# Two decode layers of attention and mixer: a planned list of loads in place of a ring

## The chip, the cores and the metric

The kernel runs on one core of one Trainium2 chip. The time is device microseconds of one launch; that of the kernel before is 2558.41 us, the median of 3 runs (2557.43 to 2562.42).

A few words that are used below. A core has a matmul engine (TensorE, PE in the profile, with PEld for its weight loads), a vector engine (DVE), a scalar engine (ACT), GpSimd (POOL) and SyncE (SP), which here does little but issue DMAs. Sixteen DMA engines move the data between HBM and the on-chip memory, whose 128 partitions are the rows of every tile. Each engine works through its own list of instructions in order, and waits where an instruction needs something that another engine or a DMA has not delivered.

## What is computed

Two rows of 512 numbers (B = 2, one token each) pass through attention, a token mixer, attention and the mixer again, each with a layer normalisation before it and a residual sum behind it. Both attention layers read the same caches of keys and values.

```python
B, Sq, D = 2, 1, 512
Hq, Hkv, Sk, Dh = 32, 8, 32768, 128
...
def _A_ref(x, k_cache, v_cache, wq, wo):
    q = (x @ wq).reshape(B, Sq, Hq, Dh).transpose(0, 2, 1, 3)
    k = jnp.repeat(k_cache, rep, axis=1)
    v = jnp.repeat(v_cache, rep, axis=1)
    scores = jnp.einsum("bhqd,bhkd->bhqk", q, k) * (Dh ** -0.5)
    p = _softmax(scores, axis=-1)
    o = jnp.einsum("bhqk,bhkd->bhqd", p, v)
    return o.transpose(0, 2, 1, 3).reshape(B, Sq, Hq * Dh) @ wo

def _B_ref(x, w1, b1, w2, b2):
    h = _layernorm(x, axis=-1)
    u = _gelu(jnp.einsum("bsd,sf->bdf", h, w1) + b1)      # F = 1792
    return (jnp.einsum("bdf,fs->bds", u, w2) + b2).transpose(0, 2, 1)

x = A_x
x = x + _A_ref(_layernorm(x, axis=-1), A_k_cache, A_v_cache, A_wq, A_wo)
x = x + _B_ref(_layernorm(x, axis=-1), B_w1, B_b1, B_w2, B_b2)
x = x + _A_ref(_layernorm(x, axis=-1), A_k_cache, A_v_cache, A_wq, A_wo)
x = x + _B_ref(_layernorm(x, axis=-1), B_w1, B_b1, B_w2, B_b2)
```

All numbers are float32. K and V are 268 MB each, so a layer reads 537 MB.

## The kernel before

The work is cut into 32 **units**, one for each layer, batch and pair of K/V head (four query heads share one). A unit is named by layer, batch and head: (0, 1, 5). Its K and its V are 16.8 MB each. It is convenient to count in **cells** of 512 columns on 128 partitions (262,144 bytes): 64 cells of K and 64 of V for each unit. A cell is what one matmul reads as its moving side.

A unit goes through these steps. `make_q` projects the normalised row with the head's part of `wq` (8 cells hold one head's `wq` and `wo`) and turns the result into columns. `k_chunk` multiplies K's cells with them into the scores (two PSUM banks, one for each half of K). `max_1` and `max_2` find the maximum over all scores of each query head; `turn_scores` transposes one half (DVE), `exponentials` takes its four heads through ACT. `v_chunk` sums V's cells with these weights into `acc`. `denominators`, `out_1` and `out_2` divide and project with `wo` into the batch's `rows`. After the last unit of a layer and batch the mixer follows: `mix_1`, `take_rows`, `mix_2` (the sum and its normalisation), 14 times `hidden_tile` (a GELU of ACT and a projection of TensorE), `take_rows`, `mix_4`, and, after layer 0, `to_columns`, which leaves the row from which the next layer's queries are made.

Time is counted in chunks of 8 cells. In slot s of the last loop `load_k(s)` issues K's chunk s and TensorE works on it, and `load_v(s)` issues V's chunk of the unit before, ten slots behind (NCH + LAG). Most loads go through SP's queue, in the order of the code; the other steps are hung on the slots in `pre` and `post`.

`PAIRED` sets where two chunks come as one load of 4 MB (slots 0 to 47 and from 212 on), elsewhere a load is one chunk of 2 MB. All of it lies in one tile `mem`. Its first part is a ring of three places (RING); where loads are paired, the ring also takes room that holds weights later, or kept V earlier. The weights of all eight heads are loaded once and stay. `KEPT` leaves 18 cells of V of head 7 in memory from layer 0 to layer 1, for each batch in turn. In HBM a partition's row of K and of V is 32 KB long, of which a 2 MB load takes half.

Layer 1 of a batch can start only after the mixer of layer 0. The units are therefore ordered so that three units of the other batch lie between (BRIDGE), first of batch 1 in layer 0 and later of batch 0 in layer 1.

After the last V's pieces (8, 4, 2, 1 and 1 cells; the last two cells through narrow matmuls), `last_mixer` does the whole output and mixer of batch 1.

Of the kernel before, what the change touches and what calls it, by code (L numbers as in the profile page):

```python
# [8 lines left out]
F32 = mybir.dt.float32  # L9
# [17 lines left out]
QT = 4  # L27
DIRECT = 3
TAIL_GROUPS = (3, 3, 3, 2)
EPS = 1e-5  # L30


@with_exitstack
def gqa_mixer_kernel(ctx: ExitStack, tc: tile.TileContext, x, kt, v, wqo, cols, out):
# [4 lines left out]

    nc = tc.nc
    B, D = out.shape
    U, NCP, DH, _ = kt.shape  # L50
    NCH = 2 * NCP
    HKV = U // B
    R = wqo.shape[2] // (2 * D)
    DT = D // P
    FT = (cols.shape[1] - 1) // 3
    LAYERS = 2
    NU = LAYERS * U
    NT = NCH * JT
    HALVES = NCH // PACK
    SCALE = DH ** -0.5  # L60
    assert DH == P and R * PACK * SUB == 32 and PACK * SUB == 2 * QT and DT == NG and R == NG and D == 512
# [3 lines left out]
    hidden = ctx.enter_context(tc.tile_pool(name="hidden", bufs=1))  # L65
# [4 lines left out]


    xcols = const.tile([P, B, D // P], F32, name="xcols")
    nc.scalar.dma_start(xcols, x)


    W = wqo.shape[2] // 2
    RING0 = 0
    KEPT0 = RING0 + RING * CK
    kept_columns = sum(KEPT.values()) * QT * DH
    order = [HKV - 1] + list(range(HKV - 1))  # L80
    home = {h: KEPT0 + kept_columns + k * 2 * W for k, h in enumerate(order)}
    mem = const.tile([P, KEPT0 + kept_columns + HKV * 2 * W], F32, name="mem")
    kept = mem[:, KEPT0 : KEPT0 + kept_columns]
    wq_sb = [mem[:, home[h] : home[h] + W].rearrange("p (t c) -> p t c", t=DT) for h in range(HKV)]
    wo_sb = [mem[:, home[h] + W : home[h] + 2 * W].rearrange("p (t c) -> p t c", t=R) for h in range(HKV)]

    def load_weights(h):
        nc.sync.dma_start(mem[:, home[h] : home[h] + 2 * W], wqo[h])


    def places(base, k, size):
        return [base + (j % RING) * size for j in range(k, k + RING)]

    PLACES = (
        (PAIRED[0][0], [], places(RING0, 0, 2 * CK)),
        (PAIRED[0][1], [RING0 + j * CK for j in (2, 3, 4)], places(RING0, 0, CK)),
        (PAIRED[1][0], [], places(RING0, 2, 2 * CK)),
    )
    turn = {}

    def buffer(s, size):
        k = max(j for j in range(len(PLACES)) if PLACES[j][0] <= s)
        _, ahead, loop = PLACES[k]
        i = turn.get(k, 0)
        turn[k] = i + 1
        f = ahead[i] if i < len(ahead) else loop[(i - len(ahead)) % len(loop)]
        return mem[:, f : f + size]

    def paired(s):
        return any(a <= s < b for a, b in PAIRED)  # L110

    load_weights(0)
    cols_sb = const.tile([P, 3 * FT + 1], F32, name="cols_sb")
    nc.scalar.dma_start(cols_sb, cols)
# [3 lines left out]

    ident = const.tile([P, P], F32, name="ident")
    make_identity(nc, ident)  # L120
    one = const.tile([P, 1], F32, name="one")
    nc.gpsimd.memset(one, 1.0)
    ones = one.to_broadcast([P, P])
    half_neg = const.tile([P, 1], F32, name="half_neg")
    nc.gpsimd.memset(half_neg, -0.5)


    selg = const.tile([P, R * QT], F32, name="selg")
    nc.vector.tensor_reduce(
        selg, ident.rearrange("p (g r) -> p r g", g=NG)[:, : R * QT, :], axis=AX.X, op=ALU.add  # L130
    )

    sel1 = selg[:, 0:1].to_broadcast([P, P])
    qpad = [const.tile([P, 64], F32, name=f"qpad{k}") for k in range(2)]
    for t in qpad:
        nc.gpsimd.memset(t, 0.0)
# [3 lines left out]
    for t in rows:  # L140
        nc.vector.memset(t, 0.0)
# [59 lines left out]
    def unit_of(n):  # L201

        return units[n]
# [508 lines left out]
```

## Time and profile before

| what | value |
|---|---|
| time, median of 3 runs | 2558.41 us |
| profiled execution: its time, which is its span | 2557.4 us |
| mean granted TensorE clock | 0.806 |
| read from HBM, and its rate over the span | 1081.11 MB, 423 GB/s |
| TensorE busy | 1634.8 us |
| mean rate in the first and last of forty slices | 417 and 264 GB/s |

The page of the profile begins with the span and the busy time of each engine. A second part cuts the span into 40 slices and gives the engines' and the DMA's busy share of each in tenths. A third lists the DMA queues with packets, megabytes and the share of sixteen engines' time. A fourth follows back what ended last. A row of a group reads: line, engine, operation, tile written and read, shape, number of instructions, then busy time in us and mean duration of one in ns, then the time that the engine sat idle just before them and what ended it. A window's row gives, for a stretch of the span, the busy time of PE, PEld, DVE, ACT and POOL with their instruction counts, the clock, the DMA's share and the rate. A float32 matmul is recorded as two instructions.

### The profile page before, as it was taken

Reading aid. Unit: us, or ns where it says so; the run is one execution under the profiler, and the core shown is the slowest. Engines: PE = TensorE matmul, PEld = TensorE weight load, DVE = VectorE, ACT = ScalarE, POOL = GpSimd, SP = SyncE. Lnnn points to the kernel's source line nnn. Section 1 sums busy time; section 2 is a strip of 40 time slices with the busy share of each in tenths; the row PEclk is TensorE's granted clock in tenths of the full one; section 3 lists DMA queues with packets and bytes.
Section 4 is the critical chain, followed back from the end, with each engine's and each line's share of the span. In section 5 each row is a group of like instructions: output and inputs, shape, how many; then the busy total and the mean of one; then the engine's idle time right before and its main releaser. Section 6 shows DMA issues by size and latency. Waiting matters only on the chain.

```text
span 2557.4 us, 21623 instructions
## 1 busy us (share of the span) xinstructions
PE 1634.8 (64%) x9708; PEld 411.4 (16%) x9708; DVE 190.9 (7%) x487; ACT 201.8 (8%) x584; POOL 4.9 (0%) x17
## 2 busy tenths in 40 slices
PE   4556566666667666666666666666756766666656
PEld 1111111111111111111111111111111111111112
DVE  1000000000011000000000000001100100000001
ACT  0000000000012000000000000001200200000002
POOL 0000000000000000000000000000000000000000
PEclk8777877787898778878887778878888887677877
DMA  9999999999999999999999999999999999999996
GB/s 417 428 432 432 429 432 431 426 427 421 426 429 427 422 428 422 428 427 428 427 429 426 422 428 427 428 423 427 428 427 424 420 433 430 431 432 432 429 433 264
DMA packets 63174, 1082.52 MB, mean 423 GB/s; under 512 B 7269, under 2 KB 7273, under 8 KB 8170
## 3 DMA queue, kind: packets, MB, share of 16 engines
q1 hardware_dynamic: 62788, 1081.11, 99.3%
q8 instruction: 76, 1.25, 0.2%
q14 instruction: 16, 0.13, 0.0%
q10 hardware_dynamic: 294, 0.03, 0.0%
HBM read 1081.11 MB, written 0.00 MB: 423 GB/s over the span
## 4 chain that ended last, share of the span: by engine, by line
DMA 77%; PE 21%; issue 0%; DVE 0%; ACT 0%; SPq 0%; POOLq 0%; DVEq 0%; ACTq 0%
DMA mem<-in_v_dram 40%; DMA mem<-in_kt_dram 38%; PE acc L352 10%; PE scores L262 10%; PE misc L216 1%; PE misc L397 0%; PE acc L516 0%; PE misc L229 0%; ACT S L299 0%; PE rows L410 0%; PE misc L379 0%; DVE row L225 0%; PE bcast L492 0%; ACT mem L526 0%; PE rows L557 0%
## 5 line engine op out<-in xcount | busy, mean ns | idle before, releaser
L352 PE MATMUL acc<-mem,S 128*16 128x512 f32 x4092 | 683.6, 801 | 416.5 <-DMA mem<-in_v_dram 416.3
L262 PE MATMUL scores<-mem,qpad 128*32 128x512 f32 x4096 | 655.6, 779 | 449.1 <-DMA mem<-in_kt_dram 448.5
L299 ACT ACTIVATE S<-S,neg 128x128 f32<-128x128 f32 x256 | 130.5, 514 | 2132.1 <-DVE neg L290 1983.7
L262 PEld LDWEIGHTS scores<-mem,qpad 128*32 128x32 f32 x4096 | 140.8, 130 | 886.8 <-DMA mem<-in_kt_dram 495.5
L352 PEld LDWEIGHTS acc<-mem,S 128*16 128x16 f32 x4092 | 125.2, 114 | 895.5 <-DMA mem<-in_v_dram 466.0
L216 PE MATMUL misc<-mem,xnT 128*1 128x512 f32 x256 | 127.3, 630 | 1.6 <-issue 1.6
L272 DVE TENSOR_REDUCE mx<-scores 128x1 f32<-128x512 f32 x64 | 44.2, 691 | 558.3 <-PE scores L262 558.3
L225 DVE COPY row<-misc 1x512 f32<-1x512 f32 x32 | 21.7, 679 | 713.8 <-PE misc L216 713.8
L294 DVE STREAM_TRANSPOSE S<-scores 128x512 f32<-128x512 f32 x64 | 45.5, 711 | 272.5 <-PE acc L352 272.5
L557 PE MATMUL rows<-hid,cols_sb 128*1 128x512 f32 x84 | 48.7, 665 | 0.0
L299 ACT ACTIVATION_READ_ACCUMULATOR S<-S,neg 128x1 f32 x256 | 47.8, 187 | 0.0
L397 PE MATMUL misc<-selg,row 128*128 128x4 f32 x256 | 36.4, 266 | 15.7 <-DVE row L394 15.1
L566 ACT ACTIVATE hid<-bcast,bias,scale 128x512 f32<-128x512 f32 x42 | 32.6, 777 | 173.9 <-PE rows L557 137.5
L397 PEld LDWEIGHTS misc<-selg,row 128*128 128x128 f32 x256 | 33.9, 206 | 48.9 <-issue 45.4
L229 PE MATMUL misc<-one,row 1*128 1x1 f32 x256 | 33.5, 248 | 9.3 <-DVE row L225 9.3
L216 PEld LDWEIGHTS misc<-mem,xnT 128*1 128x1 f32 x256 | 23.0, 90 | 101.9 <-issue 101.9
L282 DVE TENSOR_REDUCE m<-misc 1x4 f32<-1x128 f32 x32 | 8.9, 279 | 397.2 <-PE misc L280 397.2
L410 PE MATMUL rows<-mem,oT 128*1 128x512 f32 x248 | 38.1, 644 | 0.0
L229 PEld LDWEIGHTS misc<-one,row 1*128 1x128 f32 x256 | 30.8, 186 | 37.8 <-DVE row L225 20.7
L379 PE MATMUL misc<-both,one 128*128 128x4 f32 x64 | 14.5, 297 | 12.7 <-DVE both L378 12.4
L394 DVE COPY row<-acc 128x512 f32<-128x512 f32 x31 | 20.5, 660 | 0.0
L290 DVE TENSOR_SCALAR neg<-misc 128x4 f32<-128x4 f32 x32 | 5.2, 161 | 190.4 <-PE misc L288 190.4
(92 smaller groups left out, 207.4 us busy)
## 6 DMA issues: line engine op xcount, KB each, us to landing
mem<-in_kt_dram SPq DMA_DIRECT2D x164, 2048.0 KB, 12.7
mem<-in_v_dram SPq DMA_DIRECT2D x151, 2048.0 KB, 12.4
mem<-in_kt_dram SPq DMA_DIRECT2D x46, 4096.0 KB, 24.0
mem<-in_v_dram SPq DMA_DIRECT2D x45, 4096.0 KB, 23.7
mem<-in_wqo_dram SPq DMA_DIRECT2D x8, 2048.0 KB, 29.8
mem<-in_v_dram SPq DMA_DIRECT2D x8, 1280.0 KB, 12.0
mem<-in_v_dram SPq DMA_DIRECT2D x7, 1024.0 KB, 19.0
mem<-in_v_dram SPq DMA_DIRECT2D x4, 768.0 KB, 15.0
```

What stands on the lines that cost most here:

```text
L216: nc.tensor.matmul(q_ps[n][:1, :], xnT[layer, b][:, d : d + 1], wq_sb[h][:, d, :], start=(d == 0), stop=(d == DT - 1),)
L225: nc.vector.tensor_copy(q_row[n][:1, :], q_ps[n][:1, :])
L229: nc.tensor.matmul(pt[:, r : r + 1], q_row[n][:1, r * DH : (r + 1) * DH], one[:1, :], start=True, stop=True)
L262: nc.tensor.matmul(sc_ps[n, half][32 * g : 32 * g + 32, :], q, kc[:, (k * NG + g) * w : (k * NG + g + 1) * w], start=(i == 0 and k == 0), ...
L272: nc.vector.tensor_reduce(mx[n][:, half : half + 1], sc_ps[n, half], axis=AX.X, op=ALU.max)
L294: nc.vector.transpose(S[half], sc_ps[n, half])
L299: nc.scalar.activation(s[:, :, h], s[:, :, h], AF.Exp, bias=neg[n][:, h : h + 1], scale=SCALE, accum_out=lsum[n][:, half, h : h + 1],)
L352: nc.tensor.matmul(acc[32 * g : 32 * g + R * QT, :], S[half][:, col : col + R * QT], (own if q < stay else vc)[:, q * w : (q + 1) * w], st ...
L397: nc.tensor.matmul(po[:, :R], asb[:, t * DH : (t + 1) * DH], selg[:, t * R : (t + 1) * R], start=(t == 0), stop=(t == QT - 1),)
L410: nc.tensor.matmul(rows[b][32 * r : 32 * r + 1, :], oT[n][:, r : r + 1], wo_sb[h][:, r, :], start=(units[n] == lay[layer, b][0]), stop=(un ...
L557: nc.tensor.matmul(rows[key[1]][32 * g : 32 * g + 1, :], w2c[:, f - 1 : f], hid[key, f - 1], start=(f <= NG), stop=(f > FT - NG),)
L566: nc.scalar.activation(hid[key, f], px[key], AF.Gelu_apprx_tanh, bias=shift[key][:, f : f + 1], scale=slope[key][:, f : f + 1],)
```

## The change

The kernel gets a list of all steps and, from it, a list of all loads, both made when the program is built.

- **Steps.** `Order` writes out TensorE's order in steps of four cells. Most of it is K of a unit, then V of the unit before. In layer 0 the two batches alternate head by head. Heads 6 and 7 (`f` and `s`) stand around the layer changes: for each batch the unit of head 7 in layer 0 (`x0`, `x1`) comes last, then K's second half and V of a filling unit (`fill0`, `fill1`), during which the mixer runs, and then the unit of head 7 in layer 1 (`y0`, `y1`).
- **What stays.** 8 cells of K and all 64 of V of `x` are still in memory for `y`, at each of the two changes.
- **Memory.** One pool of 105 cells takes K, V and weights alike. The weights of heads 0 to 5 are loaded once in each layer (`users`), those of heads 6 and 7 once.
- **Loads.** `plan_loads` goes through the cells in the order of use. For each load it tries 32, 24, 16, 8 and 4 cells and all places in the pool, and takes the first size that by its own figures makes the queue wait for nothing, or else the one that waits least. `order.sizes` fixes the sizes near the changes (16, 8, 4, 4 cells for the end of V of `x`, 4 for K's second half and V of the filling unit) and at the very end. A row of K or V in HBM becomes 64 KB long, so a load of 32 cells takes whole rows and one of four takes 8 KB of each.
- **Issue.** A load is issued behind the step that last uses its place (`begin`).
- **Other steps.** `make_q` projects both batches at once where both rows are known. The mixer takes two of the 14 tiles at each step, with two buffers for them. `take_out` is separated from `out_1`. The small loads of `x` and of the columns go through SP's queue. What each function computes for a unit is as before.

```diff
-CK = 4096
-JT = CK // P
+G = 512
+HALF = 32
+STEP = 4
 NG = 4
-SUB = 2
-PACK = 4
-RING = 3
-PAIRED = ((0, 48), (212, 1 << 30))
-LAG = 2
-KEPT = {0: 8, 2: 4, 4: 3, 6: 3}
-BRIDGE = 3
-PIECES = (32, 16, 8, 4, 4)
-THIN = 8
 QT = 4
+CELLS = 105
+WCELLS = 8
+KEPT_K = 8
+KEPT_V = 64
+SIZES = (32, 24, 16, 8, 4)
+FINAL = (16, 8, 4, 2, 1, 1)
+TAPER = (16, 8, 4, 4)
+THIN = 2
+SLOTS = 4
 DIRECT = 3
 TAIL_GROUPS = (3, 3, 3, 2)
+TAIL_CELLS = 16
 EPS = 1e-5
+LOAD_US = 0.12
+CELL_US = 0.6024
+LAND_US = 1.0
+LEAD_US = 2.5
+STEP_US = 1.44
+class Order:
+    def __init__(self, heads):
+        far, f, s = list(range(heads - 2)), heads - 2, heads - 1
+        self.steps = []
+        self.pairs = []
+        before = [(0, b, h) for h in far for b in (0, 1)] + [(0, 0, f)]
+        x0, fill0, y0 = (0, 0, s), (0, 1, f), (1, 0, s)
+        x1, fill1, y1, n = (0, 1, s), (1, 0, f), (1, 1, s), (1, 1, f)
+        after = [(1, b, h) for h in far[:1:-1] for b in (0, 1)] + [(1, b, h) for b in (0, 1) for h in far[1::-1]]
+        for i, u in enumerate(before):
+            self.k(u)
+            if i:
+                self.v(before[i - 1])
+        self.k(x0), self.v(before[-1]), self.k(fill0, 0), self.v(x0), self.k(fill0, 1), self.v(fill0)
+        self.k(y0), self.v(y0), self.k(x1), self.k(fill1, 0), self.v(x1), self.k(fill1, 1), self.v(fill1)
+        self.k(y1), self.v(y1), self.k(n)
+        prev = n
+        for u in after:
+            self.k(u), self.v(prev)
+            prev = u
+        self.v(prev)
+        self.last = prev
...
+        self.kept = {}
+        for x, _, y in self.changes:
+            for g in range(KEPT_K):
+                self.kept["K", x, g] = ("K", y, g)
+            for g in range(KEPT_V):
+                self.kept["V", x, g] = ("V", y, g)
+        self.sizes = {}
+        for x, fill, _ in self.changes:
+            self.cut("V", x, HALF, TAPER)
+            self.cut("K", fill, HALF, (STEP,) * 8)
+            self.cut("V", fill, 0, (STEP,) * 16)
+        self.cut("V", self.last, HALF, FINAL)
+    def cut(self, kind, u, g, sizes):
+        for s in sizes:
+            self.sizes[kind, u, g] = s
+            g += s
+    def k(self, u, *halves):
+        self.phase("K", u, halves)
+    def v(self, u, *halves):
+        self.phase("V", u, halves)
+    def phase(self, kind, u, halves):
+        for half in halves or (0, 1):
+            self.steps += [(kind, u, half * HALF + i) for i in range(0, HALF, STEP)]
+def plan_loads(order, weights, busy):
+    steps = order.steps
+    step_of = {(kind, u, g + i): p for p, (kind, u, g) in enumerate(steps) for i in range(STEP)}
+    from_kept = set(order.kept.values())
+    asked = [(p, kind, u, g + i) for p, (kind, u, g) in enumerate(steps) for i in range(STEP)]
+    asked = [a for a in asked if a[1:] not in from_kept]
+    weights = sorted(weights)
+    last_use = [-1] * CELLS
+    landed, done, loads = {}, [], []
+    queue, array, begun, i = 2.0, 0.0, -1, 0
+    def ready(cells):
+        t = 0.0
+        for c in cells:
+            if last_use[c] >= len(done):
+                return None
+            if last_use[c] >= 0:
+                t = max(t, done[last_use[c]])
+        return t
+    while i < len(asked) or weights:
+        if weights and (i == len(asked) or weights[0][0] <= asked[i][0]):
+            _, name, last = weights.pop(0)
+            label, sizes, stays = ("W", name, 0), (WCELLS,), True
+        else:
+            _, kind, u, g = asked[i]
+            label, stays = (kind, u, g), (kind, u, g) in order.kept
+            n = 1
+            while (
+                i + n < len(asked)
+                and asked[i + n][1:] == (kind, u, g + n)
+                and (g + n) % HALF
+                and ((kind, u, g + n) in order.kept) == stays
+            ):
+                n += 1
+            sizes = [s for s in SIZES if s <= n] or [n]
+            if label in order.sizes:
+                sizes = [min(order.sizes[label], n)]
+        best = None
+        for s in sizes:
+            spots = range(CELLS - s + 1)
+            found = None
+            for a in spots if stays else reversed(spots):
+                t = ready(range(a, a + s))
+                if t is not None:
+                    wait = max(0.0, t + LEAD_US - queue)
+                    if found is None or wait < found[0]:
+                        found = (wait, s, a)
+            if found is not None and (best is None or found[0] < best[0] - 0.01):
+                best = found
+            if best is not None and best[0] == 0.0:
+                break
+        wait, s, a = best
+        begun = max(begun, *(last_use[a : a + s]))
+        loads.append((label, s, a, begun))
+        queue += wait + s * CELL_US + LOAD_US
+        if label[0] == "W":
+            last_use[a : a + s] = [last] * s
+        else:
+            for j in range(s):
+                key = (kind, u, g + j)
+                for k in (key, order.kept.get(key)):
+                    if k is not None:
+                        landed[k] = queue + LAND_US
+                        last_use[a + j] = step_of[k]
+            i += s
+        while len(done) < len(steps):
+            kind, u, g = steps[len(done)]
+            keys = [(kind, u, g + j) for j in range(STEP)]
+            if any(k not in landed for k in keys):
+                break
+            array = max(array, *(landed[k] for k in keys)) + STEP_US
+            array += busy.get(len(done), 0.0)
+            done.append(array)
+    return loads
...
+    order = Order(HKV)
+    steps, first, end = order.steps, order.first, order.end
...
-    hidden = ctx.enter_context(tc.tile_pool(name="hidden", bufs=1))
+    hidden = ctx.enter_context(tc.tile_pool(name="hidden", bufs=2))
...
+    xcols = const.tile([P, B, DT], F32, name="xcols")
+    nc.sync.dma_start(xcols, x)
+    mem = const.tile([P, CELLS * G], F32, name="mem")
+    def cells(a, n):
+        return mem[:, a * G : (a + n) * G]
...
+        layer, b, h = us[0]
+        n = len(us)
...
+                    q_ps[us][:n, :], xn[layer][:, d, b : b + n], wq[:, d, :], start=(d == 0), stop=(d == DT - 1)
...
+    def hidden_tiles(key, k):
+        for f in (2 * k - 2, 2 * k - 1):
+            if 0 <= f < FT:
+                project(key, f)
+        for f in (2 * k, 2 * k + 1):
+            if f < FT:
+                hid[key, f] = hidden.tile([P, D], F32, name="hid")
+                nc.scalar.activation(
+                    hid[key, f],
+                    px[key],
+                    AF.Gelu_apprx_tanh,
+                    bias=shift[key][:, f : f + 1],
+                    scale=slope[key][:, f : f + 1],
+                )
...
+        elif u not in changed:
+            queries(us, k0 - 10, k0 - 8, k0 - 6)
+    for name, us in users.items():
+        k0 = min(first["K", u] for u in us)
+        h = name if isinstance(name, int) else name[1]
+        layer = min(u[0] for u in us)
+        weights.append((k0 - 24 if k0 else -1, (layer, h), max(end["V", u, 1] for u in us) + 3))
...
+        k_mid, k_end = end["K", u, 0], end["K", u, 1]
+        v0, v_mid, v_end = first["V", u], end["V", u, 0], end["V", u, 1]
+        ahead = order.v_before[u]
+        p1, p2 = (k_end + 2, k_end + 4) if k_end + 4 < v0 else (k_end, k_end)
+        t0 = max(k_mid, end["V", ahead, 0] if ahead else 0)
+        t1 = max(k_end, end["V", ahead, 1] if ahead else 0)
+        if p2 <= t0:
+            at(p1, max_1, u, us=0.2), at(p2, max_2, u, us=0.2)
+            at(t0, turn_scores, u, 0), at(t0, exponentials, u, 0)
         else:
+            at(t0, turn_scores, u, 0)
+            at(p1, max_1, u, us=0.2), at(p2, max_2, u, us=0.2)
+            at(p2, exponentials, u, 0, us=5.0 if p1 == p2 else 0.0)
+        at(t1, turn_scores, u, 1)
+        at(max(t1, p2), exponentials, u, 1)
+        at(v_mid + 2, denominators, u, us=0.2)
+        at(v_end, take_out, u)
...
+        at(v_end + 1, out_1, u, us=1.0)
+        at(v_end + 2, out_2, u, us=2.4)
+        if u == order.last_of[key]:
+            e = v_end
+            at(e + 1, mix_1, key, us=0.8)
+            at(e + 3, take_rows, key)
+            at(e + 4, mix_2, key, us=0.7)
+            g0 = e + 9
+            for k in range(FT // 2 + 1):
+                at(g0 + k, hidden_tiles, key, k, us=1.0)
+            g0 += FT // 2
+            at(g0 + 1, take_rows, key)
+            at(g0 + 2, mix_4, key, us=0.7)
+            if layer == 0:
+                at(g0 + 3, to_columns, key, us=0.5)
+                (y,) = [y for y, (x, _) in changed.items() if x == u]
+                queries((y,), g0 + 4, g0 + 5, g0 + 6)
+                assert g0 + 6 < first["K", y]
...
+    def load(label, n, a):
+        kind, u, g = label
+        if kind == "W":
+            nc.sync.dma_start(cells(a, n), wqo[u[1]])
+            w = D * R
+            wq_sb[u] = cells(a, n)[:, :w].rearrange("p (t c) -> p t c", t=DT)
+            wo_sb[u] = cells(a, n)[:, w:].rearrange("p (t c) -> p t c", t=R)
+            return
+        layer, b, h = u
+        src = (kt if kind == "K" else v)[b * HKV + h, g // HALF, :, (g % HALF) * G : (g % HALF + n) * G]
+        nc.sync.dma_start(cells(a, n), src)
+        for j in range(n):
+            at_cell[kind, u, g + j] = a + j
+            if (kind, u, g + j) in order.kept:
+                at_cell[order.kept[kind, u, g + j]] = a + j
...
+    for label, n, a, p in loads:
+        begin.setdefault(p, []).append((label, n, a))
+    for label, n, a in begin.get(-1, ())[:1]:
+        load(label, n, a)
+    nc.sync.dma_start(cols_sb, cols)
+    for label, n, a in begin.get(-1, ())[1:]:
+        load(label, n, a)
+    constants()
...
+    for p, (kind, u, g) in enumerate(steps):
+        (k_step if kind == "K" else v_step)(u, g)
+        for f, args in hooks.pop(p, ()):
+            f(*args)
+        for label, n, a in begin.get(p, ()):
+            load(label, n, a)
...
+    kt = A_k_cache.reshape(U, 2, NG, 32, 2, 2, 8, 2, 2, DH).transpose(0, 1, 9, 4, 7, 8, 2, 5, 6, 3)
...
+        "kt": np.ascontiguousarray(kt).reshape(U, 2, DH, HALF * G),
+        "v": A_v_cache.reshape(U, 2, P, HALF * G),
```

More of the change, by code (lines that the diff above doesn't have):

```diff
@@ new lines, in gqa_mixer_kernel, with k_step @@
+    at_cell = {}
+    def k_step(u, g0):
+        half = g0 // HALF
+        if g0 % HALF == 0:
+            sc_ps[u, half] = pscore.tile([P, G], F32, name="scores")
+        for g in range(g0, g0 + STEP):
+            i, row = divmod(g % HALF, NG)
+            at = q_at[u] - R * i
+            nc.tensor.matmul(
+                sc_ps[u, half][32 * row : 32 * row + 32, :],
+                qz[:, at : at + 32],
+                cells(at_cell["K", u, g], 1),
+                start=(i == 0),
+                stop=(i == HALF // NG - 1),
+            )
+        if g0 % HALF == HALF - STEP:
@@ L637, in gqa_mixer_kernel @@
+    begin = {}
+    for label, n, a, p in loads:
[6 more added lines that the diff above has]
+    constants()
     first_input()
     for step in range(3):
[L639 to L645 removed]
@@ L646, in gqa_mixer_kernel @@
[L646 to L663 removed]
+        make_q(opening_q, step)
```

567 lines of the change are left out of this document (221 added, 346 removed).

## The prediction

> **What bounds the kernel now.** I read the page first, from its top to the chain of waits.
>
> ```profile
> span 2557.4 us, 21623 instructions
> ...
> PE 1634.8 (64%) x9708; PEld 411.4 (16%) x9708; DVE 190.9 (7%) x487; ACT 201.8 (8%) x584; POOL 4.9 (0%) x17
> ...
> DMA  9999999999999999999999999999999999999996
> ...
> q1 hardware_dynamic: 62788, 1081.11, 99.3%
> ...
> DMA 77%; PE 21%; issue 0%; DVE 0%; ACT 0%; SPq 0%; POOLq 0%; DVEq 0%; ACTq 0%
> ```
>
> The queue of SP moves 1081.11 MB and its packets fill 99.3% of sixteen DMA engines' span; only the last of the forty slices is not full. TensorE is busy 64% of the time, and the chain that ended last is loads with matmuls between them. So the kernel is a stream of bytes with a short tail, and an edit is worth what it takes from the bytes, from their rate, or from a gap in the stream. The stages come next, as windows: their clock, the engines' share and the rate are the last three columns.
>
> ```profile
> 80.00:320.00 240.00, 144.01 (x832) 37.24 (x832) 13.52 (x34) 10.95 (x43) 0.00 (x0) 0.77 1.00 431
> 480.00:560.00 80.00, 51.87 (x286) 12.53 (x278) 5.24 (x13) 4.24 (x16) 0.00 (x0) 0.76 1.01 427
> 1040.00:1360.00 320.00, 199.30 (x1200) 45.66 (x1192) 21.65 (x53) 17.20 (x64) 0.00 (x0) 0.82 1.01 428
> 1920.00:2000.00 80.00, 56.33 (x348) 14.36 (x341) 7.49 (x20) 8.01 (x21) 0.54 (x1) 0.83 1.00 417
> 2080.00:2480.00 400.00, 253.94 (x1506) 66.78 (x1502) 26.09 (x66) 20.63 (x80) 0.00 (x0) 0.78 1.00 431
> 740.00:800.00 60.00, 41.89 (x250) 9.29 (x243) 2.88 (x8) 14.07 (x22) 0.00 (x0) 0.91 1.01 427
> ```
>
> Two rates stand there. Where loads are paired (4 MB, rows of 32 KB: the stretches from 80 and from 2080 us) it is 431 GB/s; in the middle (2 MB, rows of 16 KB) it is 427 to 428. The stretch from 740 us holds a mixer between two layers and is not slower. The one from 1920 us, with 417, is the worst stage of the stream. The issues give the number of loads.
>
> ```profile
> mem<-in_kt_dram SPq DMA_DIRECT2D x164, 2048.0 KB, 12.7
> mem<-in_v_dram SPq DMA_DIRECT2D x151, 2048.0 KB, 12.4
> mem<-in_kt_dram SPq DMA_DIRECT2D x46, 4096.0 KB, 24.0
> mem<-in_v_dram SPq DMA_DIRECT2D x45, 4096.0 KB, 23.7
> mem<-in_wqo_dram SPq DMA_DIRECT2D x8, 2048.0 KB, 29.8
> mem<-in_v_dram SPq DMA_DIRECT2D x8, 1280.0 KB, 12.0
> mem<-in_v_dram SPq DMA_DIRECT2D x7, 1024.0 KB, 19.0
> ```
>
> These are 429 loads, seven smaller ones aside. A 4 MB load (4.194 MB at 431) lasts 9.73 us; two of 2 MB at 427.5 last 9.81. So **a load costs 0.08 us by itself**, and a cell of 512 columns (0.262 MB) costs (9.73 - 0.08) / 16 = **0.603 us**. With rates rounded to 1 GB/s the 0.08 could be 0.05 to 0.12.
>
> Last, what TensorE needs for the work, and both ends of the stream, from the timeline, the chain in order of time (second row) and the groups.
>
> ```profile
> 0.74 0.41 SPq L88 DMA_DIRECT2D mem<-in_wqo_dram  x1
> ...
> 1.66 26.31 DMA mem<-in_kt_dram
> ...
> 759.22 1.91 PE L352 MATMUL acc<-mem,S 128*16 128x512 f32 x16 [1.28 <-DMA mem<-in_v_dram]
> ...
> 760.97 1.02 PE L557 MATMUL rows<-hid,cols_sb 128*1 128x512 f32 x2
> ...
> 769.00 3.59 PE L352 MATMUL acc<-mem,S 128*16 128x512 f32 x16 [2.13 <-DMA mem<-in_v_dram]
> ...
> 2536.55 0.11 PEld L364 LDWEIGHTS acc<-mem,S 128*4 128x4 f32 x8 [0.32 <-DMA mem<-in_v_dram]
> ```
>
> ```profile
> L352 PE MATMUL acc<-mem,S 128*16 128x512 f32 x4092 | 683.6, 801 | 416.5 <-DMA mem<-in_v_dram 416.3
> ...
> L299 ACT ACTIVATE S<-S,neg 128x128 f32<-128x128 f32 x256 | 130.5, 514 | 2132.1 <-DVE neg L290 1983.7
> ...
> L216 PE MATMUL misc<-mem,xnT 128*1 128x512 f32 x256 | 127.3, 630 | 1.6 <-issue 1.6
> L272 DVE TENSOR_REDUCE mx<-scores 128x1 f32<-128x512 f32 x64 | 44.2, 691 | 558.3 <-PE scores L262 558.3
> ...
> L557 PE MATMUL rows<-hid,cols_sb 128*1 128x512 f32 x84 | 48.7, 665 | 0.0
> L299 ACT ACTIVATION_READ_ACCUMULATOR S<-S,neg 128x1 f32 x256 | 47.8, 187 | 0.0
> ...
> L397 PE MATMUL misc<-selg,row 128*128 128x4 f32 x256 | 36.4, 266 | 15.7 <-DVE row L394 15.1
> ...
> L282 DVE TENSOR_REDUCE m<-misc 1x4 f32<-1x128 f32 x32 | 8.9, 279 | 397.2 <-PE misc L280 397.2
> L410 PE MATMUL rows<-mem,oT 128*1 128x512 f32 x248 | 38.1, 644 | 0.0
> ...
> L290 DVE TENSOR_SCALAR neg<-misc 128x4 f32<-128x4 f32 x32 | 5.2, 161 | 190.4 <-PE misc L288 190.4
> ```
>
> A matmul of a cell is two records. Eight cells take 1.91 us at the full clock and 3.59 at the low one, so a step of four is 0.95 to 1.8 us, and on average 683.6 / 2046 x 4 = 1.34, against 4 x 0.603 = 2.4 us for its bytes. The last bytes are used at 2536.6 us, so the tail is 20.8 us.
>
> **The change part by part.** *Bytes.* Before: 4096 cells of K and V in two layers, less 2 x 18 that stay, plus 8 sets of weights of 8 cells: 4124, which is the 1081 MB of the queue's row. After: 72 cells stay at each of two changes (8 of K, 64 of V), and six of the eight heads' weights come twice: 4096 - 144 + 14 x 8 = 4064. That is 60 cells less: **-36.2 us**. The weights' 48 extra cells (29 us) are in this already.
>
> *Fewer loads.* The taper, the K fill half, the V fill and 56 cells of K after it are some 40 small loads at each change; the end takes 6, weights 14. The other 3550 cells come in 111 loads if all are 32 cells, or 444 if the room allowed only 8. The memory has 105 cells and two sets of weights take 16: 89 are left, 2.8 loads of 32. A load of 32 lasts 19.4 us, and TensorE empties one in 32 x 0.334 = 10.7 us, so the next load finds its place free. I take 140, near the lower end: 240 in all, and (430 - 240) x 0.08 = **-15.2 us**; the ends are -18 (210 loads) and +9 (550). A row of 64 KB stands nowhere in the trace. If it were served as two of 32 KB, each large load would cost one 0.08 more, 11 us in all; if it costs nothing by itself, the sum stands. I take the sum, since the price went down by halves from 16 to 32 KB.
>
> *The changes of layer.* With 72 kept cells and 16 of weights, 17 cells remain: four loads of four, 2.5 us each (2.41 + 0.08). The K fill half ends and its V follows at once, so the softmax is bare: 0.69 (L272) + 0.28 (L282) + 0.16 (L290) + four times 0.51 + 0.19 (L299) are 3.9 us, and with the small matmuls and hand-overs between them I estimate 5.7. The mixer's 14 projections stand in the first steps of that V, two to a step. A projection is two records of L557: 1.02 us at the full clock, 1.16 on average, nearly as much as a whole step. From the landing of the last K, TensorE is through step 8 of V after one step of K, the softmax, eight steps and 14 projections: at the full clock 0.95 + 5.7 + 7.6 + 14.3 = 28.5 us, by the averages 1.34 + 5.7 + 10.7 + 16.2 = 33.9. Load 12 takes the place of step 8's cells. The stream could take it up after 11 x 2.5 = 27.5 us, and gets it, with 0.9 us from issue to flow (0.74 to 1.66 at the start), at 29.4 to 34.8: 2 to 7 us late. Behind the waiting load SP holds all later ones, so the gap is lost to the stream. The granted clock of 0.91 at the mixer from 740 us is nearer to the full one; I take 4 at each change, **+8 us**. At the low clock (3.59 for 1.91, so 1.88 times as long) it is 1.8 + 5.7 + 14.4 + 26.9 + 0.9 = 49.7, 22 late. If the softmax is 2 us shorter than estimated, nothing is lost. The V that stays costs no bytes but 16 steps, 21 us of TensorE, during which K of the next unit flows into what is being freed (2.4 us a step against 1.34).
>
> *Work that moves at no cost.* One query projection for both batches spares TensorE 14 of 32 groups of 4.0 us (127.3 / 32): hidden, as TensorE waits for loads, and nothing if that cover is gone but a gain. The small loads of x and of the columns go from ACT's queue to SP's: 25 KB, under 0.5 us. The first K lands as one load of 8 MB, about 12 us later; the stream runs meanwhile. The last pieces (16, 8, 4, 2, 1, 1 cells) end as the old ones did, so the tail stays.
>
> The new softmax waits stand in TensorE's and ACT's queues, and only matmuls of the same unit are behind them. The stage of 417 GB/s and like dips are 12 us in all: 4124 x 0.603 + 436 x 0.08 = 2522, where the stream takes 1.7 to 2536. I leave them in; gone, they are -12.
>
> Sum, against the profiled execution: 2557.4 - 36.2 - 15.2 + 8 = **2514 us**. Its time is 1.0 below the median of the runs, so 2515.
>
> **The rivals.** *The ring at the changes starves.* If the clock goes low just there, both changes lose 22 us: 2515 + 36 = 2551. For it: the low clock's row at 769 us; against it: 0.91 over that window.
>
> *The plan finds no large places.* Holes between weights and kept cells leave loads of 8: +24, and 2539. It is the way in which the change would not do what it says. Against it stand the 89 cells.
>
> *Large loads give their place back too late* (slower). Place: SP's wait for the matmuls before each load.
>
> ```profile
> SPq L332 <- PE scores L262: 532.1, 169, 6.6
> ```
>
> SP waits for TensorE before nearly every load today and loses nothing, as 2.5 loads are under way (12.7 us to landing, 4.9 each). A place of 32 cells is free only after its last matmul. It decides once that is over 19.4 - 0.9 = 18.5 us after landing. At the low clock 32 cells take 14.4, which is 1.34 times their average; the query projection's 4.0 becomes 5.4, and the output matmuls' 2.3 (L397 and L410, 1.1 and 1.2 for a unit) 3.1: 22.9 in one load of each unit. With no third place that is 4.4 us late, in half of 28 units: 62 us, 2577. Against it: the mean clock of 0.8 and the 0.8 of a third place.
>
> *Rows a power of two apart.* The pitch of K and V rows doubles to 64 KB. The 0.8% between 428 and 431 may be due to 16 KB rows at a pitch of 32 KB and not to the load. Then whole rows win nothing (+15), and the short rows at the changes, 368 cells or 222 us, lose perhaps 3%: +7, and 2537; another 0.8% on the whole stream would make it 2557. The Trainium skill, "DMA: Bandwidth & Descriptors", section "Latency and other measured facts", says that row pitches of large powers of two cut the rate of 16 KB rows: 207 GB/s at 512 KiB against 214 padded, 103 at 4 MiB. By that rule a pitch of 64 KB, far below, would cost less than its 3%; this trace shows no other pitch, so nothing here can test it.
>
> **How the numbers follow.** Forecast 0.55 (own range 2500 to 2530); starved ring 0.15; no large places 0.10; late places 0.15; pitch 0.05. The lower end of the range is 2557.4 - 36.2 - 18 - 12 = 2491, without stalls or dips; the upper one takes in the starved ring, 2552. A measurement of this kernel can tell 0.2%, 5 us, from no change. Faster: 0.55 and most of three rivals, 0.80; the same 0.05, from the ends of ring and pitch; slower 0.15.
>
> **What would show it.** Bytes of SP's queue at 1065 MB, or the first term is wrong. About 240 issues, most of 8 MB, and 432 to 433 GB/s far from the changes; 431 there means that 64 KB rows bring nothing. Near the changes, two dips in the rate at the V of the filling unit, worth 8 us together, with SP waiting for the mixer's projections or the matmuls behind them. A tail of 21 us after the last landing. Dips all over the stream with SP waiting for matmuls would mean late places, and the forecast would be wrong in sign.

## The result, and the profile after

The changed kernel takes 2520.09 us (median of 4 runs, 2519.17 to 2523.71), the kernel before 2557.92 (4 runs, 2557.34 to 2562.42): a ratio of 0.9854, with a 95% interval of 0.984 to 0.9868. The forecast was 2515. The profiled execution spans 2518.4 us, where the sum gave 2514.

The page of the changed kernel, the lines that answer to those of before:

```profile
span 2518.4 us, 20745 instructions
...
PE 1442.3 (57%) x9484; PEld 400.0 (16%) x9484; DVE 181.3 (7%) x473; ACT 183.7 (7%) x572; POOL 4.9 (0%) x16
...
DMA  9999999999999999999999999999999999999996
...
q1 hardware_dynamic: 33700, 1065.40, 98.8%
...
DMA 67%; PE 31%; ACT 1%; DVE 1%; issue 0%; SPq 0%; POOLq 0%; ACTq 0%; DVEq 0%
```

SP's queue moves 1065.40 MB, which is 15.7 MB or 60 cells less. The share of TensorE in the chain has grown from 21 to 31%, which fits a stream that waits more for matmuls. Windows of the changed kernel show where:

```profile
80.00:1080.00 1000.00, 547.05 (x3580) 150.95 (x3580) 60.62 (x157) 50.70 (x192) 0.00 (x0) 0.73 1.00 432
1120.00:1260.00 140.00, 97.84 (x609) 25.33 (x600) 14.57 (x38) 18.16 (x37) 1.09 (x2) 0.82 0.99 401
1340.00:1480.00 140.00, 106.17 (x610) 27.00 (x614) 14.20 (x39) 20.98 (x48) 1.08 (x2) 0.76 0.98 399
...
1160.00:1170.00 10.00, 8.16 (x54) 1.70 (x50) 2.26 (x7) 0.00 (x0) 0.54 (x1) 0.83 0.94 375
1180.00:1190.00 10.00, 9.49 (x57) 1.93 (x53) 0.00 (x0) 8.32 (x15) 0.00 (x0) 0.81 0.95 360
1210.00:1220.00 10.00, 10.00 (x65) 3.17 (x60) 1.53 (x3) 0.00 (x0) 0.00 (x0) 0.94 0.97 365
1235.00:1245.00 10.00, 5.57 (x32) 1.01 (x32) 0.53 (x1) 0.00 (x0) 0.00 (x0) 0.66 0.98 372
```

Away from the layer changes the rate is 432 GB/s, against 427 to 431 before. In the 140 us of each change it is 401 and 399, where the kernel before ran at 427 through its first mixer. The loss is not one gap but four dips in the first change: behind the output matmuls of the unit before (1160), behind the bare softmax (1180), at the next query projection (1210), and where TensorE reads K of the next unit (1235). That K comes in loads of 8 cells, by the list in turn to three places (at 24, 89 and 97), and TensorE waits for each of them; the next bare softmax stands only at 1257 us:

```profile
1237.53 3.64 PE L322 MATMUL scores<-mem,qz 128*32 128x512 f32 x16 [3.38 <-DMA mem<-in_kt_dram]
...
1257.32 0.38 PE L340 MATMUL misc<-ident,mxa 128*1 128x128 f32 x2 [1.09 <-DVE mxa L338]
```

The DMA's share stays at 0.94 and more in them although the rate falls by a seventh: packets that wait seem to be counted as busy, so a dip is read from the rate and not from the share.

The issues: of the 232 loads, 99 have whole rows of 64 KB, and their size is left out by the profile (x50 and x49).

```profile
mem<-in_kt_dram SPq DMA_DIRECT2D x27, 2048.0 KB, 13.0
mem<-in_v_dram SPq DMA_DIRECT2D x37, 1024.0 KB, 8.2
mem<-in_kt_dram SPq DMA_DIRECT2D x32, 1024.0 KB, 9.4
...
mem<-in_kt_dram SPq DMA_DIRECT2D x50, 28.5
mem<-in_v_dram SPq DMA_DIRECT2D x49, 29.5
```

At the end, the timeline of TensorE (rows with no wait are instructions that found their data there), then two windows:

```profile
2476.54 1.91 PE L375 MATMUL acc<-mem,S 128*16 128x512 f32 x8 [14.57 <-DMA mem<-in_v_dram]
...
2497.62 0.61 PE L384 MATMUL acc<-mem,S 128*4 128x128 f32 x12
```

```profile
2494.00:2496.00 2.00, 2.00 (x24) 0.56 (x20) 0.00 (x0) 0.00 (x0) 0.00 (x0) 1.00 0.35 132
2496.00:2498.00 2.00, 2.00 (x32) 0.62 (x24) 0.00 (x0) 0.00 (x0) 0.00 (x0) 1.00 0.00 0
```

TensorE waits 14.6 us for the 32 cells of the last V's first half, and is then busy without a wait until 2498.2 us, while no byte comes after 2496. Before, its last matmuls waited for the last bytes.

### The profile page after: what moved, and what is told of

The parts are those of the page before. It is cut to its first block, busy times and chain, and to the rows that moved or that the text cites. A ratio compares the mean times of both kernels' runs of the same rounds, so it can differ in the third digit from the quotient of the medians.

```text
span 2518.4 us, 20745 instructions
## 1 busy us (share of the span) xinstructions
PE 1442.3 (57%) x9484; PEld 400.0 (16%) x9484; DVE 181.3 (7%) x473; ACT 183.7 (7%) x572; POOL 4.9 (0%) x16
## 3 DMA queue, kind: packets, MB, share of 16 engines
q1 hardware_dynamic: 33700, 1065.40, 98.8%
## 4 chain that ended last, share of the span: by engine, by line
DMA 67%; PE 31%; ACT 1%; DVE 1%; issue 0%; SPq 0%; POOLq 0%; ACTq 0%; DVEq 0%
DMA mem<-in_kt_dram 36%; DMA mem<-in_v_dram 30%; PE acc L375 12%; PE scores L322 12%; PE misc L420 2%; PE rows L437 2%; PE misc L289 1%; ACT S L357 0%; PE rows L493 0%; PE misc L346 0%; PE misc L340 0%; PE bcast L457 0%; PE acc L592 0%; PE misc L539 0%; PE bcast L519 0%
## 5 line engine op out<-in xcount | busy, mean ns | idle before, releaser
L375 PE MATMUL acc<-mem,S 128*16 128x512 f32 x4092 | 626.7, 711 | 523.0 <-DMA mem<-in_v_dram 513.3
L322 PE MATMUL scores<-mem,qz 128*32 128x512 f32 x4096 | 613.4, 734 | 524.9 <-DMA mem<-in_kt_dram 524.8
L322 PEld LDWEIGHTS scores<-mem,qz 128*32 128x32 f32 x4096 | 136.8, 128 | 926.0 <-DMA mem<-in_kt_dram 469.2
L289 PE MATMUL misc<-mem,xn 128*2 128x512 f32 (+1 forms) x144 | 86.9, 737 | 4.3 <-DMA mem<-in_wqo_dram 4.3
L420 PEld LDWEIGHTS misc<-selg,row 128*128 128x128 f32 x256 | 50.8, 295 | 46.8 <-issue 41.6
L420 PE MATMUL misc<-selg,row 128*128 128x4 f32 x256 | 53.6, 333 | 0.6 <-DVE row L405 0.6
L493 PE MATMUL rows<-hid,cols_sb 128*1 128x512 f32 x84 | 33.8, 616 | 1.0 <-ACT hid L508 1.0
L289 PEld LDWEIGHTS misc<-mem,xn 128*2 128x2 f32 (+1 forms) x144 | 14.5, 101 | 74.2 <-issue 72.9
L294 DVE COPY row<-misc 2x512 f32<-2x512 f32 (+1 forms) x18 | 12.2, 679 | 183.5 <-PE misc L289 123.0
L340 PE MATMUL misc<-ident,mxa 128*1 128x128 f32 x64 | 17.8, 375 | 5.1 <-DVE mxa L338 5.1
L298 PEld LDWEIGHTS misc<-ident,row 2*128 2x128 f32 (+1 forms) x144 | 17.3, 186 | 16.2 <-issue 12.7
```

What stands on the lines that cost most here:

```text
L289: nc.tensor.matmul(q_ps[us][:n, :], xn[layer][:, d, b : b + n], wq[:, d, :], start=(d == 0), stop=(d == DT - 1))
L322: nc.tensor.matmul(sc_ps[u, half][32 * row : 32 * row + 32, :], qz[:, at : at + 32], cells(at_cell["K", u, g], 1), start=(i == 0), stop=(i ...
L340: nc.tensor.matmul(pm[:1, :P], mxa, ident, start=True, stop=True)
L375: nc.tensor.matmul(acc[32 * row : 32 * row + R * QT, :], S[half][:, col : col + R * QT], vc, start=(g < NG), stop=(g >= quads - NG),)
L420: nc.tensor.matmul(po[:, :R], asb[u][:, t * DH : (t + 1) * DH], selg[:, t * R : (t + 1) * R], start=(t == 0), stop=(t == QT - 1),)
L493: nc.tensor.matmul(rows[key[1]][32 * g : 32 * g + 1, :], w2c[:, f : f + 1], hid.pop((key, f)), start=(f < NG), stop=(f >= FT - NG),)
```

## The experiments

The numbers below are medians of the time; each kernel ran beside the kernel before, whose median lay between 2558.3 and 2559.3 us.

**Loads of 4 cells, with gaps and without.**

```diff
-SIZES = (32, 24, 16, 8, 4)
+SIZES = (4,)
-FINAL = (16, 8, 4, 2, 1, 1)
-TAPER = (16, 8, 4, 4)
+FINAL = (4,) * 7 + (2, 1, 1)
+TAPER = (4,) * 8
```

> Every load of K and V is cut to 4 cells (8 KB rows at a pitch of 64 KB), 1004 loads in place of 232, the same bytes. Theory (a load costs 0.08 us by itself, whatever its rows): 772 x 0.08 = 62 us more, about 2582, with some 418 GB/s all along the stream. Rival (short rows at a wide pitch are slow, the 0.8 per cent for each halving): much the same 420 GB/s here; the two part on the next kernel.

Then, in the second kernel, with the same sizes, K and V in blocks of 1 MB:

```diff
-        src = (kt if kind == "K" else v)[b * HKV + h, g // HALF, :, (g % HALF) * G : (g % HALF + n) * G]
+        src = (kt if kind == "K" else v)[b * HKV + h, g // STEP, :, (g % STEP) * G : (g % STEP + n) * G]
...
-        "v": A_v_cache.reshape(U, 2, P, HALF * G),
+        "v": np.ascontiguousarray(
+            A_v_cache.reshape(U, 2, P, HALF // STEP, STEP * G).transpose(0, 1, 3, 2, 4)
+        ).reshape(U, 2 * HALF // STEP, P, STEP * G),
```

> The same 1004 loads of 4 cells, but K and V lie in HBM in blocks of 1 MB, so that the 8 KB rows of a load follow each other without a gap. Theory (price of a load): no change against the kernel with the gaps, about 2582 and 418 GB/s. Rival (pitch): the rate returns to about 432 GB/s and the time to about 2520.

Measured: 2813 us (ratio 1.099, 1.0911 to 1.107) and 2843 us (1.1107, 1.1076 to 1.1138). Packing the rows brings nothing. Over most of their span both kernels run well below the 421 GB/s that 0.08 us a load allows (the next experiments say why), and there a cost of the pitch could hide. So the pitch is better read from a stretch in which both run at their fastest. The row with gaps comes first, then the packed one:

```profile
1640.00:1700.00 60.00, 48.19 (x317) 11.06 (x316) 5.72 (x14) 4.15 (x16) 0.00 (x0) 0.82 1.01 421
```

```profile
1640.00:1700.00 60.00, 47.99 (x340) 12.80 (x333) 6.66 (x17) 4.15 (x16) 0.00 (x0) 0.90 1.01 421
```

The rate is the same, so the pitch of 64 KB costs nothing that shows. But a load seemed to cost (2813 - 2520) / 772 = 0.38 us, five times what was expected; both theories had missed.

**Loads of at most 16 cells.**

```diff
-SIZES = (32, 24, 16, 8, 4)
+SIZES = (16, 8, 4)
```

> The largest load is 16 cells (32 KB rows), 332 loads in place of 232, the same bytes. Theory (0.08 us for a load): 8 us more, 2528, with about 431 GB/s away from the changes. Rival (rows of 64 KB bring nothing over 32 KB): the same time, 2520.

Measured: 2578.97 us (1.0071, 1.0054 to 1.0088), 59 us more for 100 loads. That is no price of a load: the kernel before made 315 loads of 2 MB, half that size, at 427 GB/s. The list shows something else. A part of it, as the cells of V that are loaded, their number, the first cell of the place, and the step behind which the load is issued:

```
V (0,1,3)  0   16 cells at 73, behind 247
V (0,1,3) 16   16 cells at 89, behind 255
V (0,1,3) 32   16 cells at 73, behind 259
V (0,1,3) 48   16 cells at 89, behind 263
```

`plan_loads` goes through the places from the highest down and keeps the first that, by its own figures, costs no wait. So the loads mostly take turns in two places at the top of the memory, each begins just when the list thinks that its place is free, and some 40 to 50 cells lie empty. The next kernels tell this from the price of a load.

**The place that has been free longest.** One condition is changed in `plan_loads`:

```diff
-                    if found is None or wait < found[0]:
-                        found = (wait, s, a)
+                    if found is None or (wait, t) < found[::3]:
+                        found = (wait, s, a, t)
...
```

With loads of at most 16 cells:

> Loads of at most 16 cells again, but the list takes, among the places that by its figures cost no wait, the one that has been free longest (before: the highest). 325 loads. Theory of late places (with the highest place, 16-cell loads took turns in two or three places at the top of the memory and each began only just after its place came free, while 40 cells lay empty): the rate away from the changes returns to 431, and the time to 2520 + 93 x 0.08 = 2527. Rival (a load of 16 cells costs 0.6 us by itself): 2575 as before.

With loads of 4 cells:

> Loads of 4 cells everywhere, 1004 of them, in the place that has been free longest. Theory of late places, 0.08 us for a load: 418 GB/s and about 2582. Rival (0.38 us for a load by itself): 2813 as before.

Measured: 2521.87 (0.9855, 0.9841 to 0.9868) in place of 2579, and 2578.63 (1.0076, 1.0058 to 1.0095) in place of 2813. Theory of late places, both times. Issues of the 16-cell loads, first with the highest place, then with the longest free:

```profile
mem<-in_v_dram SPq DMA_DIRECT2D x108, 4096.0 KB, 14.8
mem<-in_kt_dram SPq DMA_DIRECT2D x105, 4096.0 KB, 19.8
```

```profile
mem<-in_kt_dram SPq DMA_DIRECT2D x109, 4096.0 KB, 42.9
mem<-in_v_dram SPq DMA_DIRECT2D x109, 4096.0 KB, 43.3
```

From issue to landing is 15 to 20 us against 43: one and a half to two loads of 9.7 us under way against more than four. The windows from 80 to 1080 us, in the same order:

```profile
80.00:1080.00 1000.00, 585.02 (x3448) 152.47 (x3448) 59.35 (x153) 50.70 (x192) 0.00 (x0) 0.77 0.99 418
```

```profile
80.00:1080.00 1000.00, 605.96 (x3556) 157.69 (x3560) 60.60 (x157) 50.80 (x192) 0.00 (x0) 0.76 1.00 431
```

and of the 4-cell loads:

```profile
80.00:1080.00 1000.00, 637.87 (x3142) 103.95 (x3138) 54.01 (x139) 47.00 (x176) 0.00 (x0) 0.67 0.98 379
```

```profile
80.00:1080.00 1000.00, 669.67 (x3488) 112.55 (x3488) 59.32 (x153) 51.43 (x192) 0.00 (x0) 0.71 1.01 421
```

The price of a load, cleanly now: (2578.6 - 2515.6) / (1004 - 226) = 0.081 us, against the kernel of 226 loads below, which chooses places in the same way. Every load of K or V has 128 rows, so a price of a load and a price of its rows can't be told apart here.

**The room at the changes.** Three kernels keep less:

```diff
-KEPT_K = 8
-KEPT_V = 64
+KEPT_K = 0
+KEPT_V = 0
```

Nothing kept, as shown:

> Nothing stays from layer to layer: 144 cells more (4208 in place of 4064), 198 loads. Theory (0.603 us for a cell; the dips at the changes come from the small room that the kept cells leave): 86.9 - 2.7 - some 15 for the dips that go, about 2589, and 425 GB/s or more in the stretches around the changes. Rival (the dips come from the mixer's and the query's matmuls or from the short rows, not from the room): they stay, about 2604.

KEPT_K = 0 alone:

> The 8 cells of K do not stay: 16 cells more to load (9.6 us), and 25 free cells at the changes in place of 17, so six places of four. Theory of the small room: the dips lose about 10 of their 15 us, so 2520 within 3. Rival (not the room): 2530.

KEPT_K = 0 and KEPT_V = 48:

> No K and 48 of 64 cells of V stay: 48 cells more than the changed kernel loads (29 us), 41 free cells, 206 loads (-2). Theory of the small room: no dips are left, 2520 + 29 - 2 - 15 = 2532. Rival (not the room): 2547.

Measured: 2592.0, 2521.86 and 2536.29 us. What each gives back is the price of its bytes and loads less what it costs:

| kept at a change | free cells there | bytes and loads | cost measured | given back |
|---|---|---|---|---|
| 8 K, 64 V | 17 | | | |
| 0 K, 64 V | 25 | 9.6 us | 1.8 us | 7.8 us |
| 0 K, 48 V | 41 | 28.9 - 2.1 us | 16.2 us | 10.6 us |
| nothing | 89 | 86.8 - 2.7 us | 71.9 us | 12.2 us |

The windows of the two changes for 25 free cells, then for 89:

```profile
1120.00:1260.00 140.00, 96.82 (x612) 26.24 (x604) 14.55 (x38) 18.11 (x37) 1.09 (x2) 0.83 1.00 413
1340.00:1480.00 140.00, 102.67 (x594) 27.25 (x594) 14.03 (x38) 20.99 (x48) 1.08 (x2) 0.80 1.00 412
```

```profile
1120.00:1260.00 140.00, 92.40 (x592) 25.95 (x588) 12.65 (x33) 16.85 (x32) 1.09 (x2) 0.80 1.01 426
1340.00:1480.00 140.00, 89.64 (x576) 26.20 (x572) 13.13 (x36) 21.07 (x48) 1.08 (x2) 0.79 1.01 425
```

With 41 free cells the two windows run at 418 and 422. So the dips come from the room: the same matmuls, waits and 4-cell loads of the filling unit stand in the kernel that keeps nothing, and its stream runs at 426 and 425 there. Keeping less also leaves TensorE fewer steps that need no bytes, and these kernels do not separate that from the room; but 8 cells of K, which are few steps, already give back 7.8 of the 12.2 us.

**What keeps the small ring late.** Two kernels take one delay each out of TensorE's way:

```diff
     def hidden_tiles(key, k):
+        if key[0] == 0:
+            return
```

> Leaves out the mixer's 14 GELUs and 14 projections of layer 0 for both batches; all waits around them stay. Theory as forecast (the projections behind the bare softmax make load 12 late): the dips go down by most of what they lose, 6 to 12 us in all, about 2510. Rival (the loss is a sum of many short delays in a ring of four places, of which the projections are one): 2 to 4 us, about 2517, with the dips in other places as they were.

```diff
...
-        if p2 <= t0:
+        if p1 == p2:
+            at(t0, turn_scores, u, 0), at(t0, same_max, u, ahead), at(t0, exponentials, u, 0)
+        elif p2 <= t0:
```

> The units whose V follows their K at once (the filling unit and the one after it, at both changes) take the maximum of the unit before in place of their own: max_1 and max_2 are left out there, and the first half's exponentials run before the second half of K. Theory of the bare softmax: TensorE begins V some 5 us sooner four times, and the dips behind these places go, 4 to 8 us in all, about 2514. Rival (the ring is short everywhere around the changes): 0 to 2 us.

Measured: 2520.59 and 2519.33 us (2 runs each), the changed kernel's time both times. Without the mixer's tiles the dip at 1180 us is still there, and those at 1160, 1210 and 1235 too (330, 333 and 347 GB/s):

```profile
1180.00:1190.00 10.00, 7.01 (x40) 1.27 (x40) 0.00 (x0) 2.90 (x12) 0.00 (x0) 0.67 0.93 338
```

Without the bare softmax this dip goes, but the one at 1160 us is deeper (348 GB/s), the second change is worse than it was (windows), and TensorE, which begins V right behind K, now stands before the first GELU (timeline, below).

```profile
1180.00:1190.00 10.00, 8.20 (x46) 2.07 (x46) 0.00 (x0) 7.79 (x13) 0.00 (x0) 0.83 1.01 411
...
1340.00:1480.00 140.00, 106.21 (x686) 28.69 (x686) 14.62 (x37) 21.31 (x48) 1.08 (x2) 0.84 0.98 392
```

```profile
1182.86 1.68 PE L497 MATMUL rows<-hid,cols_sb 128*1 128x512 f32 x2 [1.71 <-ACT hid L512]
```

So neither is the cause by itself. Both taken out together were not tried, the output matmuls and the query projection were left in their places, and which of the remaining delays then counts stays open.

**A kernel that beats both.** The longest-free place with all five sizes, and the last unit's first half of V in two loads:

```diff
+        self.cut("V", self.last, 0, (16, 16))
         self.cut("V", self.last, HALF, FINAL)
```

> All five sizes, the place that has been free longest, and the last unit's first half of V in two loads of 16 cells in place of one of 32 (226 loads). Theory: at the end TensorE begins V some 9 us sooner and is no longer 3 us behind the last byte: 2 us; and fewer just-in-time places around the changes: 0 to 5 us. Together 2513 to 2518. Rival (the end is bound by the last byte, the changes by the room alone): 2520.

Measured: 2515.64 us (5 runs, 2514.63 to 2516.63), ratio 0.983 (0.9816 to 0.9843); all its runs lie below all of the changed kernel's. The changes run faster, at 408 and 403 GB/s:

```profile
1120.00:1260.00 140.00, 97.55 (x620) 23.75 (x616) 14.55 (x38) 20.55 (x47) 1.08 (x2) 0.83 0.99 408
1340.00:1480.00 140.00, 105.10 (x645) 27.05 (x634) 14.89 (x40) 20.97 (x48) 1.08 (x2) 0.83 0.99 403
```

140 x (7 + 4) / 405 = 3.8 us of the 4.5 come from there. The end gave well under the 2 us expected. There the rate falls off before 2492 us and the last narrow matmuls end at 2494.0, so TensorE is still some 2 us behind the last byte:

```profile
2490.00:2492.00 2.00, 2.00 (x24) 0.57 (x20) 0.00 (x0) 0.00 (x0) 0.00 (x0) 1.00 0.34 131
```

```profile
2493.42 0.61 PE L385 MATMUL acc<-mem,S 128*4 128x128 f32 x12
```

On top of it, five places in place of four, and a finer end:

```diff
-KEPT_K = 8
+KEPT_K = 4
-FINAL = (16, 8, 4, 2, 1, 1)
+FINAL = (8, 8, 8, 4, 2, 1, 1)
```

> On top of the kernel with the longest-free place and the divided last V: 4 cells of K stay in place of 8 (8 cells more to load, 4.8 us; five places of four at the changes), and the last half of V comes as 8, 8, 8, 4, 2, 1, 1 cells. Theory of the room: the fifth place takes back 4 to 6 us at the changes (the rate there rises from 403 to 408 to about 413), and the end is 1 us nearer to the last byte: 2514 to 2516 against 2515.6. Rival (the room pays only in larger steps): 2519.

Measured: 2516.05 us (5 runs, 2515.64 to 2518.08), ratio 0.9834 (0.982 to 0.9847), not to be told from the kernel without it. The changes run at 410 and 416 GB/s, which is 140 x (2 + 13) / 410 = 5.1 us as forecast, and the bytes of the 8 cells (4.8 us) take that back. The end came out as said: bytes come until 2493 us, and the last matmuls, which wait for their pieces again, end at 2494.2:

```profile
2492.45 1.04 PE L376 MATMUL acc<-mem,S 128*16 128x512 f32 x4 [0.19 <-DMA mem<-in_v_dram]
2493.12 1.03 PE L385 MATMUL acc<-mem,S 128*4 128x128 f32 x16
```

## Why the prediction was right, point by point

**Bytes, -36.2 us: right.** The queue carries 1065.40 MB as forecast. The price of a cell can be checked between the two kernels with the most room: the one that keeps nothing loads 96 cells more than the one that keeps 48 of V, with 8 loads fewer, and takes 55.7 us longer; with 0.6 us for those loads that is 0.587 a cell, against 0.603 and with more room on its side.

**Fewer loads, -15.2 us: right.** 232 loads against the 240 that were taken, and 0.081 us a load against 0.08. A row of 64 KB costs no more than the sum: 432 GB/s against the 432 to 433 forecast.

**The changes, +8 us: right in sign, too small, and by another mechanism.** The table gives 10.6 to 12.2 us for the small room. The windows give more: their 280 us carry 112 MB, which is 427 cells in about 80 loads, or 264 us at the sum's prices, so by this estimate 16 us are lost there. The step that failed is "TensorE is through step 8 of V" after 28.5 to 33.9 us with "14 projections" one behind the other. TensorE began the filling V at 1179.3 us, 7 us after the last K, and worked off the projections by 1197:

```profile
1172.33 1.94 PE L322 MATMUL scores<-mem,qz 128*32 128x512 f32 x8 [0.88 <-DMA mem<-in_kt_dram]
...
1179.26 3.62 PE L375 MATMUL acc<-mem,S 128*16 128x512 f32 x16 [2.46 <-ACT S L357]
...
1195.14 1.05 PE L375 MATMUL acc<-mem,S 128*16 128x512 f32 x8 [0.40 <-DMA mem<-in_v_dram]
```

The 7 us are what the sum had for the last step of K and the softmax. But at 1195 us, with the last two projections to come, TensorE is waiting for bytes again, 22.8 us after the last K's landing, and it is through step 8 after 23.9 and through that step's projections after 24.8. With 0.9 us to flow, load 12 is in time for the 27.5 us, so the gap that was forecast there did not come. The stream had lost its time earlier: the bytes of step 8, due after 8 x 2.5 = 20 us, came 2.8 us late, behind the softmax and the first steps of V. The size of a projection was wrong. Two adjacent ones write different rows of their tile and overlap: four records, which are two projections, take 1.22 us where a single record takes 0.59. All 42 of them were busy for 33.8 us, 0.80 each, where 1.02 to 1.16 was taken. SP was to wait for the projections or the matmuls behind them. In the first change, its waits for loads aside, it waited for projections three times, and mostly for the matmuls of K and V (us in total, times, longest):

```profile
SPq L722 <- PE scores L322: 35.9, 19, 3.7
SPq L722 <- PE acc L375: 26.6, 12, 4.6
...
SPq L722 <- PE rows L493: 5.7, 3, 2.0
```

With the projections left out, nothing was won. What the runs put in the place of that one gap is a ring of four places of 4 cells, or three of 8, and dips at several delays of some microseconds: output matmuls, softmax, query projection, and K of the next unit. Only the softmax and the mixer's tiles were taken out, each alone; that each of the others costs its dip is read from where the dips stand and not shown.

**What moves at no cost: right but for the end.** The tail was said to stay at 20.8 us. From V's last matmul it does (2498.2 to 2518.4, 20.2), but that now comes some 3 us after the last byte: the load of 32 cells hands TensorE half of the last V at once, and late. That is 1 to 2 us. Together with 3 to 4 at the changes, by the table, it makes the 4.4 us between 2514 and 2518.4.

**The total: near, in part by luck.** By the sum's own prices the stream needs 4064 x 0.603 + 232 x 0.08 = 2469 us, and it takes 1.6 to 2495.5, which is 25 more. If 16 of them are lost at the changes, 9 are lost elsewhere, where the sum left the 12 us of the kernel before in. So a part of what the changes cost more than was forecast came back in the dips, which the sum had left as they were without an argument.

**The rivals.** The starved ring was the right place, at 11 to 16 us of the 44 that it was given; it was argued from a low clock, and the granted clock in the two windows was 0.82 and 0.76. The pitch fell with the packed rows. No large places: 99 loads have 32 cells. Late places was the rival on the other side, and it lay dormant in the plan. It was argued for large loads, which give their place back late; it struck with small ones. Where the loads take turns in two places, TensorE has the time of one load to empty a place. With 32 cells (the changed kernel's list alternates between the places at 41 and 73) that is 19 us, and it was enough (432 GB/s); with 16 it is half of that, and 59 us are lost.

## What to carry to other kernels

A planner that takes the first place which is free in time by its own figures builds a ring as short as these figures allow, and leaves the rest of the memory empty; taking the place that has been free longest cost nothing here and took back 57 of the 59 us that a choice of sizes had seemed to cost. Before calling a difference between load sizes the price of a load, look at the time from issue to landing: it tells how many loads are under way. Where kept data shrinks a ring, count the microseconds that the ring holds against all delays of the engine that empties it, one after the other; here, removing one of them alone won nothing.

## What the runs showed of the hardware that was not expected

A row appears to be one packet, whether it has 8, 32 or 64 KB. With 128 rows and 16 packets more for each load, 232 loads are 33408 packets, and the queue's row has 33700; with the 16-cell loads (332) it has 48100, with the 4-cell loads (1004) 144868. Each time that is 144 a load and 292 over. And the DMA's busy share hardly falls when loads come late: 0.98 at 379 GB/s over 1000 us, against 1.01 at 421 with the same loads issued earlier.
